# Linear attention with two gated layers: q of blocks 1 to 5 loaded in 32x32 pieces and transposed by VectorE

## The chip, the cores and the metric

The kernel runs on one core of a Trainium2 chip. The metric is the device time of one execution in microseconds. The engines are TensorE (PE, with its weight loads as PEld), VectorE (DVE), ScalarE (ACT), GpSimd (POOL) and SyncE (SP), whose queue issues all the transfers of this kernel.

## The reference

For each of 4 batches and 8 heads, k and v give a 64 x 64 matrix, q is multiplied by it, and each row is normed. The result is a matrix x of 2304 tokens x 512, which goes through a layer with a gate and then through a product of two layers:

```
kv  = einsum('bhsd,bhse->bhde', k, v)              # q, k, v: 4 x 8 x 576 x 64, float32
out = einsum('bhsd,bhde->bhse', q, kv)
out = out / sqrt(mean(out * out, -1) + 1e-6) * g_norm
x   = out.transpose(0, 2, 1, 3).reshape(2304, 512)
h   = x @ w_in;  x1 = (h * sigmoid(h)) @ w_out      # 512 -> 2048 -> 512
y   = ((x1 @ w_a) * (x1 @ w_b)) @ w_out2            # 512 -> 1536 -> 512
```

The weights come as float64 and are decoded on the chip.

## The kernel before, in words

The tokens are cut into 6 blocks of 384 (three chunks of 128). The matrix products are done at full float32 precision by splitting each operand into a high and a low part and adding three products.

A weight tile of w_in or w_out (names wi0 to wi15 and wo0 to wo15) is loaded raw (load_w, L265), scaled by ScalarE (dec_scale, L279), shifted and joined by VectorE (dec_shift L285, dec_low L291, dec_sign L298), and split into the high part (ScalarE, L307) and the low part (GpSimd or VectorE, L313).

For each block and each of 4 pairs of heads, q has to lie with the head's dimension along the partitions, since TensorE contracts over partitions. load_q (L123) loads a chunk of 128 tokens with all 8 heads, one token to a partition, in runs of 64 floats. stage_a1 (L173) has TensorE transpose the three chunks of a pair into PSUM (qtp), and stage_a2 (L180) has ScalarE copy them to SBUF (qT). stage_b (L189) multiplies qT by kvc, the matrices of k and v (ao); then come the norm (L201 to L218) and a second transpose, x, which is split into xh and xl (L224 to L240). Block 0 loads its q in another way (load_q_first, L134).

A step of the main loop (step1, L399) is one hidden tile of one block: 12 matmuls for h (hp, L328), the gate (ScalarE's sigmoid L388, VectorE's product L393), the split of the gate into gh and gl (L338, L343), and the 12 matmuls of the step before into x1 (x1p, L354). Work of the next block, the decoding of weights and the loads hang on steps (the table `side`, filled by `at`, L738); a step's extra work follows its x1 on each engine. VISITS (L42) says which hidden tiles of which block follow each other, and base[i] is the first step of visit i. q of block 2 is transposed in steps 19, 21, 23 and 25, q of blocks 3, 4 and 5 in the steps base[5], base[6] and base[7] plus 1, 4, 7 and 10.

The opening is written out by hand. LOADS (L23) is the order of the first loads in SP's queue: `q3 q4 q5` are the chunks of block 1, `k11` is k and v of batch 1 and pair 1, `t1` their last 64 tokens, `wi1` a raw weight tile. ORDER (L27) is the order of the items on all the engines: `A:1:2` is stage_a1 of block 1 and pair 2, `a:1:2` its stage_a2, `c`, `s`, `j`, `k`, `p`, `P` are the steps of a weight's decoding, `K` and `O` make kvc, `H` is a part of h, `G`, `g`, `S`, `t` gate and split, `X` is x1. Each engine works its instructions off in this order, and an instruction that waits holds up all that stand behind it on its engine.

Buffers: `page` is a pool of 37 tiles of 4 KB per partition, `small` one of 6 tiles of 2 KB.

Of the kernel before, what the change touches and what calls it, by code (L numbers as in the profile page):

```python
# [8 lines left out]
F32 = mybir.dt.float32  # L9
# [6 lines left out]
P = 128  # L16
CH = 3
TB = CH * P
# [2 lines left out]


LOADS = """  # L23
k02 Q t0 k00 k01 g k03 wi1 wi0 q3 q4 wo0 q5 wo1 k11 k10 t1 wi2 wo2 wo3 wi3 k13 k12"""


ORDER = """  # L27
W:11 Q:1 Q:0 Q:2 W:1 A:0:2 K:0:2 A:0:1 A:0:3 K:0:0 a:0:2 O:0:2:0 O:0:2:1 A:0:0 B:0:2 O:0:0:0 a:0:3 O:0:0:1 a:0:0
K:0:1 B:0:0 a:0:1 n:0:2 r:0:2 K:0:3 n:0:0 O:0:1:0 c:wi1 O:0:1:1 O:0:3:1 w:0:2 r:0:0 m:0:2 s:wi1 B:0:1 O:0:3:0 w:0:0
n:0:1 B:0:3 n:0:3 r:0:1 m:0:0 w:0:1 r:0:3 w:0:3 W:7 j:wi1 d:0:2 m:0:1 k:wi1 c:wi0 d:0:0 W:4 x:0:2 s:wi0 d:0:1 p:wi1  # L30
m:0:3 x:0:1 P:wi1 d:0:3 x:0:0 x:0:3 j:wi0 k:wi0 p:wi0 c:wo0 H:1:0:4 l:0:0 P:wi0 H:1:4:8 A:1:2 A:1:1 l:0:1 a:1:1
H:0:0:4 l:0:2 l:0:3 c:wo1 H:1:8:12 A:1:0 H:0:4:8 H:0:8:12 a:1:0 G:1 G:0 s:wo0 j:wo0 A:1:3 s:wo1 k:wo0 g:1 a:1:2
K:1:0 j:wo1 p:wo0 k:wo1 a:1:3 p:wo1 g:0 S:1 P:wo0 O:1:0:0 O:1:0:1 K:1:1 O:1:1:1 O:1:1:0 B:1:0 S:0 P:wo1 c:wi2 t:1
B:1:1 t:0 X:0:0 n:1:0 X:0:1 s:wi2 j:wi2 n:1:1 r:1:0 w:1:0 c:wo2 k:wi2 c:wo3 r:1:1 X:0:2 X:1:0 p:wi2 s:wo3 w:1:1
X:1:1 X:1:2 P:wi2 s:wo2 m:1:0 d:1:0 H:2:0:4 c:wi3 j:wo3 m:1:1 s:wi3 d:1:1 x:1:0 l:1:0 H:2:4:8 K:1:3 j:wi3 k:wo3
# [6 lines left out]
VISITS = [(0, 0, 4), (1, 0, 8), (0, 4, 12), (1, 8, 16), (0, 12, 16),  # L42
          (2, 0, 16), (3, 0, 16), (4, 0, 16), (5, 0, 16)]
# [16 lines left out]
def tile_linattn_moe_moe2(ctx: ExitStack, tc: tile.TileContext, q, k, v, g_norm,  # L60
                          w_in, w_out, w_a, w_b, w_out2, out):
    nc = tc.nc
    B, H, S, D = q.shape
# [22 lines left out]
    first = tc.alloc_tile_pool(name="first", bufs=1)  # L86
# [2 lines left out]
        return sb.tile(shape, dt, tag="page", bufs=NPAGE, name=name)  # L89

    def small(shape, dt, name):
        return first.tile(shape, dt, tag="small", bufs=6, name=name)

    def mid(shape, dt, name):
        return sb.tile(shape, dt, tag="mid", bufs=6, name=name)
# [10 lines left out]
    qs, qT, xn, ao, rms, xt = {}, {}, {}, {}, {}, {}  # L106
    xh, xl = {}, {}

    def load_kv(b, p):
        t = page([P, 2, 2, 4 * D], F32, f"kv_{b}_{p}")  # L110
        for i, src in enumerate((k, v)):
            nc.sync.dma_start(
                t[:, i], src[b, 2 * p:2 * p + 2, 0:4 * P, :].rearrange("h (p c) d -> p h (c d)", c=4))
        kvp[b, p] = t

    def load_kvt(b):
        t = page([P, 2, H, D], F32, f"kvt_{b}")
        nc.gpsimd.memset(t[ST:], 0.0)
        for i, src in enumerate((k, v)):
            nc.sync.dma_start(t[0:ST, i], src[b, :, 4 * P:S, :].rearrange("h p d -> p h d"))  # L120
        kvt[b] = t

    def load_q(c):  # L123

        t = (page if c < 2 * CH else small)([P, H, D], F32, f"q_{c}")
        done = 0
        while done < P:
            b, t0 = divmod(c * P + done, S)
            n = min(P - done, S - t0)
            nc.sync.dma_start(t[done:done + n], q[b, :, t0:t0 + n, :].rearrange("h p d -> p h d"))  # L130
            done += n
        qs[c] = t

    def load_q_first():  # L134

        t = six([P, H, CH, D], F32, "q_first")
        nc.sync.dma_start(t.rearrange("p h c d -> p h (c d)"),
                          q[0, :, 0:TB, :].rearrange("h (p c) d -> p h (c d)", c=CH))
        qs["first"] = t
# [31 lines left out]
    bufs = {"at": 2, "h": 2, "acc": 4}  # L171

    def stage_a1(j, p, tag="at"):  # L173

        pt = ps.tile([P, TB], F32, tag=tag, bufs=bufs[tag], name=f"qtp_{j}_{p}")
        for i in range(CH):
            nc.tensor.transpose(pt[:, i * P:(i + 1) * P], qs[j * CH + i][:, 2 * p:2 * p + 2, :], ident)  # L177
        qT[j, p] = pt

    def stage_a2(j, p):  # L180
        t = mid([P, TB], F32, f"qT_{j}_{p}")
        nc.scalar.copy(t, qT[j, p])
        qT[j, p] = t

    def stage_a(j, p):
        stage_a1(j, p)
        stage_a2(j, p)

    def stage_b(j, p, tag="at"):  # L189

# [60 lines left out]
    def load_w(key):  # L251
        kind, f = key
        fs = slice(f * P, (f + 1) * P)
        src = srcs[kind]
        wide = src.dtype != F32
        if kind in ("wi", "wa", "wb"):
            src = src[:, fs]
        else:
            src = src[fs, :]
        if wide:  # L260
            src = src.bitcast(U32)
        if kind in ("wi", "wa", "wb"):
            src = src.rearrange("(kt p) f -> p kt f", p=P)
        r = page([P] + list(src.shape[1:]), U32 if wide else F32, f"raw_{kind}{f}")
        nc.sync.dma_start(r, src)  # L265
        raws[key] = r.rearrange("p k f -> p (k f)") if kind in ("wi", "wa", "wb") else r
# [43 lines left out]
    def dec_rest(key, eng=None):  # L310
        m = mids.pop(key)
        hi, lo = W[key]
        (eng or nc.gpsimd).tensor_sub(lo, m, hi.bitcast(F32))  # L313
# [6 lines left out]
    acc, part, gg = {}, {}, {}  # L320
# [410 lines left out]
    base = []  # L731
    n = 0
# [5 lines left out]
    def at(g, fn, *args):  # L738
        side.setdefault(g, []).append(lambda: fn(*args))
# [20 lines left out]

    v4 = base[4]
    for p in range(NP):
        at(v4 - 9 + 2 * p, stage_a, 2, p)
        at(v4 - 8 + 2 * p, attend, 2, p)
        at(-(v4 - 7 + 2 * p), norm_mul, 2, p)
        at(v4 + p // 2, stage_d, 2, p)
    for vi in range(5, 8):
        j = VISITS[vi][0] + 1
        for p in range(NP):
            at(-(base[vi] + 3 + 3 * p), norm_mul, j, p)  # L770
            at(base[vi] + 1 + 3 * p, stage_a, j, p)
            at(base[vi] + 2 + 3 * p, attend, j, p)
            at(base[vi] + 4 + 3 * p, stage_d, j, p)
    for i in range(CH):
        at(v4 - 12 + i, load_q, 2 * CH + i)
        for vi in range(5, 8):
            at(base[vi] - 3 + i, load_q, (VISITS[vi][0] + 1) * CH + i)

    early = {}
# [111 lines left out]
    def load_g():  # L893
        nc.sync.dma_start(g2[0:D], g_norm.unsqueeze(1))
        nc.sync.dma_start(g2[D:P], g_norm.unsqueeze(1))

    for name in LOADS.split():
        if name == "g":
            load_g()
        elif name == "Q":  # L900
            load_q_first()
        elif name[0] == "t":
            load_kvt(int(name[1]))
        elif name[0] == "k":
            load_kv(int(name[1]), int(name[2]))
        elif name[0] == "q":
            load_q(int(name[1]))
        else:
            load_w((name[:2], int(name[2:])))

# [2 lines left out]
    def item(name):  # L913
        kind, *r = name.split(":")
        if kind in "csjkpPyL":
            key = (r[0][:2], int(r[0][2:]))
            if kind == "L":
                load_w(key)
            elif kind == "y":
                dec_rest(key, nc.vector)  # L920
            else:
                {"c": dec_scale, "s": dec_shift, "j": dec_low, "k": dec_sign, "p": dec_high,
                 "P": dec_rest}[kind](key)
            return
        r = [int(e) for e in r]
        early = r[0] == 0
        if kind == "W":
            warm(*r)
        elif kind == "Q":
            unpack_q(*r)  # L930
        elif kind == "K":
            kv_mm(*r)
        elif kind == "O":
            kv_out(*r)
        elif kind == "A":
            stage_a1(*r, "acc" if early else "at")
        elif kind == "a":
            stage_a2(*r)
        elif kind == "B":
            stage_b(*r, "acc" if early else "at")  # L940
        elif kind == "n":
            norm_square(*r)
        elif kind == "r":
            norm_mean(*r)
        elif kind == "w":
            norm_root(*r)
        elif kind == "m":
            norm_mul(*r)
        elif kind == "d":
            stage_d1(*r, "acc" if early else "at")  # L950
        elif kind == "x":
            stage_d2(*r)
        elif kind == "l":
            stage_d3(*r)
        elif kind == "H":
            f, n0, n1 = r
            if n0 == 0:
                hp[f] = ps.tile([P, TB], F32, tag="h", bufs=2, name=f"hp_0_{f}")
            h_part(hp[f], 0, "wi", f, n0, n1)
        elif kind == "G":  # L960
            gate1(0, r[0], hp[r[0]])
        elif kind == "g":
            gate2(0, r[0], hp[r[0]])
        elif kind == "S":
            gg[0, r[0]] = [split_high(hg[0, r[0]], f"0_{r[0]}")]
        elif kind == "t":
            gg[0, r[0]].append(split_low(hg.pop((0, r[0])), gg[0, r[0]][0], f"0_{r[0]}"))
        elif kind == "X":
            f, i = r
            if f == 0 and i == 0:  # L970
                acc[0] = [ps.tile([P, TB], F32, tag="acc", bufs=4, name=f"x1p_0_{c}") for c in range(KD)]
            for c in range(KD):
                x1_part(0, f, c, i)

    with tc.manual_schedule():
# [7 lines left out]
        g = base[1]  # L983
# [14 lines left out]
        for n, (d, p) in enumerate(seq):  # L998
            new = 0 < n < NPAIR
            if NPAIR + 1 <= n <= NPAIR + 4:  # L1000

                kt, h = divmod(n - NPAIR - 1, 2)
# [50 lines left out]
```

## Time and profile before

| | us |
|---|---|
| median of 3 runs | 881.38 (880.87 to 881.59) |
| span of the profiled execution, from the first to the last instruction | 879.4 |
| TensorE busy in the span | 869.5 |
| VectorE busy | 595.9 |
| ScalarE busy | 318.2 |
| GpSimd busy | 50.7 |

The profile gives the profiled execution as its span; a time that it took from outside is not told apart from the three runs. The first 45 us of the span are the opening, in which the DMA engines are busy over 90% of the time (the page's first two slices of 22 us). The main loop of the gate layer follows, then the product of the two layers.

### The profile page before, as it was taken

The numbers are of one execution on the slowest core, as the hardware profiler recorded it, in microseconds if no ns is written. First come the engines' busy times: TensorE is split into PE (matmuls) and PEld (weight loads), VectorE is DVE, ScalarE is ACT, GpSimd is POOL, SyncE is SP. The second block draws the span as 40 slices with busy tenths as digits, with TensorE's granted clock in tenths as the row PEclk, the third lists the DMA queues.
The fourth block names the chain that finished last, engine by engine and source line by source line (L and its number), as shares of the span: only waits on it lengthen the run. The fifth ranks groups of instructions, "written<-read, shape, count | busy, mean of one in ns | idle before, by whom it ended". The sixth has DMA issues, their size and how long they took to land.

```text
span 879.4 us, 13480 instructions
## 1 busy us (share of the span) xinstructions
PE 869.5 (99%) x5111; PEld 828.9 (94%) x5111; DVE 595.9 (68%) x1115; ACT 318.2 (36%) x648; POOL 50.7 (6%) x53
## 2 busy tenths in 40 slices
PE   8999999999999999999999999999999999999998
PEld 5799999999999999999999999999999999999996
DVE  4889786454677678888755677776656665535555
ACT  4766554343444445455442422221222211121110
POOL 4410002010101000100000000000000000000000
PEclk9999999999999999999999999999999999999999
DMA  9960244044463565558999967276788476765001
GB/s 296 368 246 1 73 140 112 1 134 157 139 218 139 182 201 186 195 220 292 407 367 374 360 238 263 97 271 256 249 289 287 132 274 240 286 216 193 1 0 72
DMA packets 99185, 179.67 MB, mean 204 GB/s; under 512 B 26544, under 2 KB 68016, under 8 KB 99120
## 3 DMA queue, kind: packets, MB, share of 16 engines
q1 hardware_dynamic: 99120, 178.81, 57.7%
q8 instruction: 40, 0.66, 0.3%
q14 instruction: 25, 0.20, 0.1%
HBM read 127.66 MB, written 51.12 MB: 203 GB/s over the span
## 4 chain that ended last, share of the span: by engine, by line
PE 96%; DVE 1%; DMA 1%; ACT 1%; issue 0%; POOL 0%; SPq 0%; DVEq 0%; ACTq 0%
PE hp L328 23%; PE x1p L354 22%; PE op L710 17%; PE X_a L632 4%; PE V_a L632 4%; PE Z_a L632 4%; PE X_b L632 4%; PE Z_b L632 4%; PE V_b L632 4%; PE Y_b L632 2%; PE Y_a L632 2%; PE ao L197 2%; DMA kv<-in_v_dram 1%; PE kvps L159 1%; PE qtp L177 1%; PE xtp L231 1%
## 5 line engine op out<-in xcount | busy, mean ns | idle before, releaser
L354 PE MATMUL x1p<-gh,wo 128*128 128x384 f32 x768 | 193.4, 335 | 0.0
L328 PE MATMUL hp<-xh,wi 128*128 128x384 f32 x768 | 154.7, 342 | 0.4 <-ACT xh L235 0.3
L354 PEld LDWEIGHTS x1p<-gh,wo 128*128 128x128 f32 x768 | 138.4, 188 | 0.0
L328 PEld LDWEIGHTS hp<-xh,wi 128*128 128x128 f32 x768 | 132.9, 188 | 1.6 <-ACT xh L235 1.0
L354 PE MATMUL x1p<-gl,wo 128*128 128x384 f32 x384 | 127.4, 335 | 0.0
L388 ACT ACTIVATE g<-hp 128x384 f32<-128x384 f32 x96 | 47.2, 491 | 113.7 <-PE hp L328 113.6
L393 DVE TENSOR_TENSOR g<-hp,g 128x384 f32<-128x384 f32 x96 | 53.3, 555 | 49.4 <-ACT g L388 49.0
L710 PE MATMUL op<-wp,ab 128*128 128x512 f32 x360 | 83.4, 390 | 0.0
L328 PE MATMUL hp<-xl,wi 128*128 128x384 f32 x384 | 82.4, 335 | 0.0
L710 PEld LDWEIGHTS op<-wp,ab 128*128 128x128 f32 x360 | 67.4, 188 | 13.7
L684 ACT CAST ab<-a 128x384 fp32r<-128x384 f32 x72 | 37.0, 514 | 115.1 <-DVE a L678 58.1
L343 DVE TENSOR_TENSOR gl<-g,gh 128x384 fp32r<-128x384 f32 x96 | 54.7, 570 | 31.3 <-ACT gh L338 27.4
L338 ACT CAST gh<-g 128x384 fp32r<-128x384 f32 x96 | 49.3, 514 | 67.5 <-DVE g L393 67.4
L718 DVE TENSOR_TENSOR o<-op,o 128x512 f32<-128x512 f32 x90 | 60.3, 686 | 17.6 <-PE op L710 17.5
L354 PEld LDWEIGHTS x1p<-gl,wo 128*128 128x128 f32 x384 | 71.9, 188 | 0.0
L328 PEld LDWEIGHTS hp<-xl,wi 128*128 128x128 f32 x384 | 67.9, 188 | 0.3 <-DVE xl L239 0.3
L710 PE MATMUL op<-w,ab 128*128 128x512 f32 x288 | 66.9, 390 | 0.0
L710 PEld LDWEIGHTS op<-w,ab 128*128 128x128 f32 x288 | 53.9, 188 | 10.9
L213 POOL TENSOR_TENSOR rr<-ss,nhalf 128x6 f32<-128x6 f32 x24 | 34.4, 1438 | 297.1 <-DVE ss L208 297.0
L632 PE MATMUL X_a<-xc,wp 128*128 128x384 f32 x216 | 43.8, 337 | 0.0
L632 PE MATMUL Z_a<-xc,wp 128*128 128x384 f32 x216 | 43.3, 335 | 0.0
L632 PE MATMUL V_a<-xc,wp 128*128 128x384 f32 x216 | 43.3, 335 | 0.0
(137 smaller groups left out, 1249.4 us busy)
## 6 DMA issues: line engine op xcount, KB each, us to landing
wp<-wd SPq DMA_DIRECT2D x114, 512.0 KB, 6.1
xc<-xcd SPq DMA_DIRECT2D x21, 768.0 KB, 7.4
raw_wi<-in_moe_w_in_dram SPq DMA_DIRECT2D x16, 512.0 KB, 7.6
raw_wo<-in_moe_w_out_dram SPq DMA_DIRECT2D x16, 512.0 KB, 7.3
raw_wa<-in_moe_w_a_dram SPq DMA_DIRECT2D x12, 512.0 KB, 5.9
raw_wb<-in_moe_w_b_dram SPq DMA_DIRECT2D x12, 512.0 KB, 5.9
wd<-s_wa SPq DMA_DIRECT2D x12, 512.0 KB, 3.3
wd<-s_wb SPq DMA_DIRECT2D x12, 512.0 KB, 3.3
```

The source lines that it names most:

```text
L197: nc.tensor.matmul(o[a:e, i], t[:, i * P + a:i * P + e], kvc[bb, p], start=True, stop=True)
L213: nc.gpsimd.tensor_tensor(r, rms[j, p], nhalf, op=ALU.pow)
L328: nc.tensor.matmul(o, w[wp][:, kt * P:(kt + 1) * P], x[key][:, kt, :], start=(n == 0), stop=(n == 3 * KD - 1))
L338: nc.scalar.copy(gh, src)
L343: nc.vector.tensor_sub(gl, src, gh.bitcast(F32))
L354: nc.tensor.matmul(acc[vi][c], w[wp][:, c * P:(c + 1) * P], gg[vi, s][g], start=(s == s0 and i == 0), stop=(s == s1 - 1 and i == 2))
L388: nc.scalar.activation(g, o, AF.Sigmoid)
L393: nc.vector.tensor_mul(g, o, g)
L632: nc.tensor.matmul(b[bank], w_part(p, mat, name, wq, kt), xc[d, i][:, xq, kt, :], start=(fresh and k == 0), stop=(k == 5), skip_group_chec ...
L684: nc.scalar.copy(o[:, 0], t)
L710: nc.tensor.matmul(o, ab[d, p, f, n][:, g, ts], wp[p, 7 + f][:, wq * DM:(wq + 1) * DM], start=(k == 0), stop=(k == 5))
L718: nc.vector.tensor_add(t, o, t)
```

## The change

q of blocks 1 to 5 is no longer loaded by chunks. For each pair of heads (r = 0, 1) and each half of the head's dimension, one part of a tile qb is loaded into 32 partitions: partition i of a part gets the tokens i, i + 32, i + 64, ... and of each 32 floats. VectorE's transpose turns each 32x32 block, and the result has the head's dimension along the partitions and the tokens in order along the row, as qT had it. A part is cut where the block crosses from one batch to the next, which blocks 1 and 4 do. q of block 0 stays as it was, and the function stage_a is gone.

```
 LOADS = """
-k02 Q t0 k00 k01 g k03 wi1 wi0 q3 q4 wo0 q5 wo1 k11 k10 t1 wi2 wo2 wo3 wi3 k13 k12"""
+k02 Q t0 k00 k01 g k03 wi1 wi0 b2 b1 wo0 b0 b3 wo1 k11 k10 t1 wi2 wo2 wo3 wi3 k13 k12"""
...
-m:0:3 x:0:1 P:wi1 d:0:3 x:0:0 x:0:3 j:wi0 k:wi0 p:wi0 c:wo0 H:1:0:4 l:0:0 P:wi0 H:1:4:8 A:1:2 A:1:1 l:0:1 a:1:1
+m:0:3 x:0:1 P:wi1 d:0:3 x:0:0 x:0:3 j:wi0 k:wi0 p:wi0 c:wo0 H:1:0:4 l:0:0 P:wi0 H:1:4:8 l:0:1 a:1:1
...
-        return first.tile(shape, dt, tag="small", bufs=6, name=name)
+        return first.tile(shape, dt, tag="small", bufs=3, name=name)
...
+    def load_q_blocks(j, p):
+        t = first.tile([P, TB // 32, 32], F32, tag="qb", bufs=4, name=f"qb_{j}_{p}")
+        for part in range(4):
+            r, half = divmod(part, 2)
+            done = 0
+            while done < TB:
+                b, t0 = divmod(j * TB + done, S)
+                n = min(TB - done, S - t0)
+                nc.sync.dma_start(
+                    t[part * 32:part * 32 + 32, done // 32:(done + n) // 32, :],
+                    q[b, 2 * p + r, t0:t0 + n, half * 32:half * 32 + 32].rearrange("(t i) d -> i t d", i=32))
+                done += n
+        qs["blocks", j, p] = t
+
+    def turn_q(j, p):
+        qT[j, p] = mid([P, TB], F32, f"qT_{j}_{p}")
+        nc.vector.transpose(qT[j, p], qs.pop(("blocks", j, p)).rearrange("p t d -> p (t d)"))
...
-        at(v4 - 9 + 2 * p, stage_a, 2, p)
+        at(v4 - 9 + 2 * p, turn_q, 2, p)
...
-            at(base[vi] + 1 + 3 * p, stage_a, j, p)
+            at(base[vi] + 1 + 3 * p, turn_q, j, p)
...
-    for i in range(CH):
-        at(v4 - 12 + i, load_q, 2 * CH + i)
+    for i in range(4):
+        at(v4 - 13 + i, load_q_blocks, 2, i)
         for vi in range(5, 8):
-            at(base[vi] - 3 + i, load_q, (VISITS[vi][0] + 1) * CH + i)
+            at(base[vi] - 4 + i, load_q_blocks, VISITS[vi][0] + 1, i)
...
-            stage_a2(*r)
+            stage_a2(*r) if early else turn_q(*r)
```

On SP's queue in the opening, between the raw tiles of w_in and k and v of batch 1, this stood before (the last number of a name is the tile's, and 128x8x64 means partitions, heads and floats):

```order
L265 DMA raw_wi1_121<-in_moe_w_in_dram 128x4x256
L265 DMA raw_wi0_123<-in_moe_w_in_dram 128x4x256
L130 DMA q_3_125<-in_q_dram 128x8x64
L130 DMA q_4_127<-in_q_dram 64x8x64 x2
L265 DMA raw_wo0_130<-in_moe_w_out_dram 128x1024
L130 DMA q_5_132<-in_q_dram 128x8x64
L265 DMA raw_wo1_134<-in_moe_w_out_dram 128x1024
L112 DMA kv_1_1_136<-in_k_dram 128x2x256
L112 DMA kv_1_1_136<-in_v_dram 128x2x256
```

This stands there now (32x6x32 means partitions, runs and floats; the line numbers are those of the changed kernel):

```order
L269 DMA raw_wi1_121<-in_moe_w_in_dram 128x4x256
L269 DMA raw_wi0_123<-in_moe_w_in_dram 128x4x256
L132 DMA qb_1_2_125<-in_q_dram 32x6x32 x8
L132 DMA qb_1_1_134<-in_q_dram 32x6x32 x8
L269 DMA raw_wo0_143<-in_moe_w_out_dram 128x1024
L132 DMA qb_1_0_145<-in_q_dram 32x6x32 x8
L132 DMA qb_1_3_154<-in_q_dram 32x6x32 x8
L269 DMA raw_wo1_163<-in_moe_w_out_dram 128x1024
L112 DMA kv_1_1_165<-in_k_dram 128x2x256
L112 DMA kv_1_1_165<-in_v_dram 128x2x256
```

Four transfers of q became 32, and raw_wo1 and all that follows stand behind them.

On VectorE in the opening, from block 0's xl (the low part of x) to the gate's low parts gl, this stood before:

```order
L239 SCALAR_TENSOR_TENSOR xl_0_317<-xtp_0_1_328,g2_64,xh_0_316 128x384
L239 SCALAR_TENSOR_TENSOR xl_0_317<-xtp_0_2_307,g2_64,xh_0_316 128x384
L239 SCALAR_TENSOR_TENSOR xl_0_317<-xtp_0_3_338,g2_64,xh_0_316 128x384
L285 TENSOR_SCALAR m_wo0_348<-m_wo0_348 128x512
L291 SCALAR_TENSOR_TENSOR m_wo0_348<-raw_wo0_130,m_wo0_348 128x512
L285 TENSOR_SCALAR m_wo1_379<-m_wo1_379 128x512
L298 SCALAR_TENSOR_TENSOR m_wo0_348<-raw_wo0_130,m_wo0_348 128x512
L393 TENSOR_TENSOR g_0_1_399<-hp_0_1_350,g_0_1_399 128x384
L291 SCALAR_TENSOR_TENSOR m_wo1_379<-raw_wo1_134,m_wo1_379 128x512
L298 SCALAR_TENSOR_TENSOR m_wo1_379<-raw_wo1_134,m_wo1_379 128x512
L393 TENSOR_TENSOR g_0_0_401<-hp_0_0_372,g_0_0_401 128x384
L343 TENSOR_TENSOR gl_0_1_462<-g_0_1_399,gh_0_1_434 128x384
```

This stands there now, from the shift of wo1 on:

```order
L140 STREAM_TRANSPOSE qT_1_0_414<-qb_1_0_145 128x384
L289 TENSOR_SCALAR m_wo0_377<-m_wo0_377 128x512
L295 SCALAR_TENSOR_TENSOR m_wo0_377<-raw_wo0_143,m_wo0_377 128x512
L289 TENSOR_SCALAR m_wo1_400<-m_wo1_400 128x512
L302 SCALAR_TENSOR_TENSOR m_wo0_377<-raw_wo0_143,m_wo0_377 128x512
L397 TENSOR_TENSOR g_0_1_416<-hp_0_1_379,g_0_1_416 128x384
L140 STREAM_TRANSPOSE qT_1_2_425<-qb_1_2_125 128x384
L295 SCALAR_TENSOR_TENSOR m_wo1_400<-raw_wo1_163,m_wo1_400 128x512
L302 SCALAR_TENSOR_TENSOR m_wo1_400<-raw_wo1_163,m_wo1_400 128x512
L140 STREAM_TRANSPOSE qT_1_3_442<-qb_1_3_154 128x384
L397 TENSOR_TENSOR g_0_0_418<-hp_0_0_393,g_0_0_418 128x384
L347 TENSOR_TENSOR gl_0_1_475<-g_0_1_416,gh_0_1_447 128x384
```

The four transposes stand among block 0's xl (one, not in these rows), ahead of the shift of wo0 (one) and behind the shift of wo1 (two). On TensorE and ScalarE the groups of three transposes and the copies of blocks 1 to 5 are gone and nothing else moved.

In the stage of block 4 the 32 pieces stand on SP's queue between raw_wb0, raw_wb1 and raw_wa2, raw_wa3, with four stores of decoded weights (wd) among them, where four transfers of q stood.

## Rows read from the trace of the kernel before

**Rows 1.** The page's busy times: engine, us (share of the span), instructions.

```profile
PE 869.5 (99%) x5111; PEld 828.9 (94%) x5111; DVE 595.9 (68%) x1115; ACT 318.2 (36%) x648; POOL 50.7 (6%) x53
```

**Rows 2.** The chain that ended last: share of the span by engine.

```profile
PE 96%; DVE 1%; DMA 1%; ACT 1%; issue 0%; POOL 0%; SPq 0%; DVEq 0%; ACTq 0%
```

**Rows 3.** TensorE's timeline, 107 to 118.5 us: start, us, engine, line, what.

```profile
109.24 0.50 PE L354 MATMUL x1p<-gh,wo 128*128 128x384 f32 x2
...
113.41 0.50 PE L354 MATMUL x1p<-gh,wo 128*128 128x384 f32 x2
...
115.48 0.49 PE L177 MATMUL qtp<-ident,q 128*128 128x128 f32 x3
...
117.90 0.50 PE L354 MATMUL x1p<-gh,wo 128*128 128x384 f32 x2
```

**Rows 4.** Groups by form: count | busy us, mean ns | idle before, releaser.

```profile
L208 DVE TENSOR_REDUCE ss<-sq 128x6 f32<-128x390 f32 x24 | 13.4, 557 | 16.1 <-ACT sq L203 16.1
...
L177 PE MATMUL qtp<-ident,q 128*128 128x128 f32 x72 | 11.8, 277 | 0.9 <-DVE q L147 0.8
...
L182 ACT COPY qT<-qtp 128x384 f32<-128x384 f32 x24 | 11.2, 475 | 2.6 <-PE qtp L177 2.4
```

**Rows 5.** VectorE's timeline, 237 to 242 us.

```profile
238.18 0.56 DVE L343 TENSOR_TENSOR gl<-g,gh 128x384 fp32r<-128x384 f32 x1
```

**Rows 6.** TensorE's timeline, 237 to 242 us.

```profile
240.10 0.34 PE L354 MATMUL x1p<-gl,wo 128*128 128x384 f32 x1
```

**Rows 7.** SP's queue in the opening: start of issue, us that it took, what.

```profile
9.60 4.84 SPq L130 DMA_DIRECT2D q<-in_q_dram  x3
...
15.96 1.16 SPq L265 DMA_DIRECT2D raw_wo<-in_moe_w_out_dram  x1
```

**Rows 8.** SP's queue at 92, 124 and 246 us: three forms of load.

```profile
92.36 0.37 SPq L130 DMA_DIRECT2D q<-in_q_dram  x1
...
124.06 0.62 SPq L120 DMA_DIRECT2D kvt<-in_k_dram  x1
...
246.15 1.32 SPq L130 DMA_DIRECT2D q<-in_q_dram  x2
```

**Rows 9.** DMA issues at 16.0 and 59.7 us: count, KB, us to landing.

```profile
raw_wo<-in_moe_w_out_dram SPq DMA_DIRECT2D x1, 512.0 KB, 6.6
...
raw_wo<-in_moe_w_out_dram SPq DMA_DIRECT2D x1, 512.0 KB, 3.5
```

**Rows 10.** ScalarE's timeline, 20 to 32 us: start, us, what [idle before, releaser].

```profile
23.71 0.67 ACT L279 ACTIVATE m_wo<-raw_wo 128x512 f32<-128x512 f32 x1
25.18 0.48 ACT L182 COPY qT<-qtp 128x384 f32<-128x384 f32 x1 [0.80 <-PE qtp L177]
...
26.61 0.49 ACT L388 ACTIVATE g<-hp 128x384 f32<-128x384 f32 x1 [0.56 <-PE hp L328]
```

**Rows 11.** VectorE's timeline, 20 to 32 us.

```profile
29.33 2.13 DVE L343 TENSOR_TENSOR gl<-g,gh 128x384 fp32r<-128x384 f32 x2 [0.75 <-ACT gh L338]
31.39 0.41 DVE L285 TENSOR_SCALAR m_wi<-m_wi 128x512 uint32<-128x512 uint32 x1
```

**Rows 12.** TensorE's timeline, 26 to 32.5 us.

```profile
29.66 2.29 PE L197 MATMUL ao<-kvc,qT 128*128 128x128 f32 x16 [0.44 <-ACT kvc L167]
31.70 1.11 PE L354 MATMUL x1p<-gh,wo 128*128 128x384 f32 x5
```

**Rows 13.** SP's queue, 238 to 252.8 us.

```profile
238.54 1.04 SPq L265 DMA_DIRECT2D raw_wb<-in_moe_w_b_dram  x2
...
251.01 1.65 SPq L265 DMA_DIRECT2D raw_wa<-in_moe_w_a_dram  x2
```

**Rows 14.** ScalarE's timeline, 268 to 270 us.

```profile
268.29 1.23 ACT L279 ACTIVATE m_wa<-raw_wa 128x512 f32<-128x512 f32 x2
```

**Rows 15.** The run's end by stretches: busy us by engine, PEclk the granted clock.

```profile
870.00:877.00 7.00, 5.52 (x25) 4.24 (x23) 3.46 (x5) 0.00 (x0) 0.00 (x0) 1.00 0.48 187
...
877.80:879.30 1.50, 0.00 (x0) 0.00 (x0) 0.00 (x0) 0.00 (x0) 0.00 (x0) 0.50 0.01 1
```

More of the change, by code (lines that the diff above doesn't have):

```diff
@@ L30 @@
 n:0:1 B:0:3 n:0:3 r:0:1 m:0:0 w:0:1 r:0:3 w:0:3 W:7 j:wi1 d:0:2 m:0:1 k:wi1 c:wi0 d:0:0 W:4 x:0:2 s:wi0 d:0:1 p:wi1
-m:0:3 x:0:1 P:wi1 d:0:3 x:0:0 x:0:3 j:wi0 k:wi0 p:wi0 c:wo0 H:1:0:4 l:0:0 P:wi0 H:1:4:8 A:1:2 A:1:1 l:0:1 a:1:1
-H:0:0:4 l:0:2 l:0:3 c:wo1 H:1:8:12 A:1:0 H:0:4:8 H:0:8:12 a:1:0 G:1 G:0 s:wo0 j:wo0 A:1:3 s:wo1 k:wo0 g:1 a:1:2
+m:0:3 x:0:1 P:wi1 d:0:3 x:0:0 x:0:3 j:wi0 k:wi0 p:wi0 c:wo0 H:1:0:4 l:0:0 P:wi0 H:1:4:8 l:0:1 a:1:1
+H:0:0:4 l:0:2 l:0:3 c:wo1 H:1:8:12 H:0:4:8 H:0:8:12 a:1:0 G:1 G:0 s:wo0 j:wo0 s:wo1 k:wo0 g:1 a:1:2
 K:1:0 j:wo1 p:wo0 k:wo1 a:1:3 p:wo1 g:0 S:1 P:wo0 O:1:0:0 O:1:0:1 K:1:1 O:1:1:1 O:1:1:0 B:1:0 S:0 P:wo1 c:wi2 t:1
@@ L121, in load_kvt @@
         kvt[b] = t
[L123 to L132, printed above, removed]
+    def load_q_blocks(j, p):
[14 more added lines that the diff above has]
+        nc.vector.transpose(qT[j, p], qs.pop(("blocks", j, p)).rearrange("p t d -> p (t d)"))
     def load_q_first():
@@ L183, in stage_a2 @@
         qT[j, p] = t
-    def stage_a(j, p):
-        stage_a1(j, p)
-        stage_a2(j, p)
     def stage_b(j, p, tag="at"):
@@ L905, in tile_linattn_moe_moe2 @@
             load_kv(int(name[1]), int(name[2]))
-        elif name[0] == "q":
-            load_q(int(name[1]))
+        elif name[0] == "b":
+            load_q_blocks(1, int(name[1]))
         else:
@@ L935, in item @@
         elif kind == "A":
-            stage_a1(*r, "acc" if early else "at")
+            stage_a1(*r, "acc")
         elif kind == "a":
-            stage_a2(*r)
+            stage_a2(*r) if early else turn_q(*r)
         elif kind == "B":
```

## The prediction

> **What bounds the kernel now.** I read the page first: TensorE is busy 99% of the span [rows 1], and the chain that ended last is TensorE for 96% of it [rows 2]. So time taken off TensorE comes off the end wherever nothing else is late, and time added elsewhere costs only where TensorE is made to wait. Then I read TensorE's timeline, which shows what one group of q transposes costs, then the timelines of SyncE's queue (SP), ScalarE and VectorE in the first 35 us, the one stretch where the other engines set TensorE's pace, and last the stage in which q of block 4 is loaded, because a queue that gets more transfers must be looked at wherever it gets them. The span of the profiled execution is 879.4 us and the median of the runs 881.4; I take the 2.0 us between them as unchanged, so a change of the span is added to 881.4.
>
> **What goes from TensorE.** A plain step of the gate/up loop, from one start of x1 to the next, lasts 113.41 - 109.24 = 4.17 us. The next step, which ends in the three transposes of one pair of heads, lasts 117.90 - 113.41 = 4.49 us [rows 3]. A group of three thus costs TensorE 0.32 us, not three times the 277 ns of one instruction, since neighbours overlap [rows 4]. The change removes 20 groups: 16 of blocks 2 to 5, in stages where TensorE has no other wait, and 4 of block 1 in the opening. The 16 give 16 x 0.32 = 5.1 us. The 4 would give 1.3 us, but they stand ahead of a wait that the change lengthens (below), so I count nothing for them.
>
> **What goes from ScalarE.** 20 copies of 475 ns [rows 4], all at places where TensorE does not wait for them except in the opening; nothing is counted.
>
> **What VectorE gets.** 20 transposes of 128x384. None is in this trace. The nearest rows are one-source instructions of the same width, 557 ns (the reduction, 128x390) [rows 4]; the ends I keep are 0.41 us, the shift over 512 columns [rows 11], and 1.11 us, twice the reduction. I take 0.56, or 0.47 start to start as its neighbours have it. In blocks 2 to 5 each stands in a step's tail, ahead of the next gate. The tightest place I found there is gl, which ends at 238.74 and is first read at 240.10: 1.36 us to spare [rows 5, 6]. That holds even 1.11 us, so the 16 cost nothing. If that cover were gone, each would cost TensorE what exceeds it.
>
> **What SyncE gets.** This is the term that decides. q of block 1 was 4 transfers; it is 32 now (4 pairs x 4 parts, and each part is cut in two where the batch changes at token 576), each of 32 partitions x 6 x 128 bytes, 24 KB. One queue issues them in order, between raw_wi0 and raw_wo1, and everything behind raw_wo1 (k and v of batch 1, the next weights) is pushed back with it. What does one issue cost? q in 128 partitions took 0.37 us when it was alone; kvt, in 64 partitions, 0.62; the q halves in 64 partitions 1.32 for two, 0.66 each [rows 8]. So fewer partitions are no cheaper here, they are dearer, although half the bytes move. For 32 partitions the trace has no row: below is 0.37 + 0.05 between issues = 0.42, above is one more step of 0.29 on top of 0.66, 0.95 + 0.05 = 1.0. I take 0.66 with the gap, the row of the same function with the smallest transfer.
>
> The opening with that: the issue of the pieces begins at 9.60, where the first q load was issued [rows 7]. 32 x 0.66 = 21.1 us, and raw_wo0 between them 0.5 (1.04 for two) [rows 13]: raw_wo1 is issued at 31.2 instead of 15.96 [rows 7]. It then landed 6.6 us after its issue, in a full queue; a raw_wo in an empty one took 3.5 [rows 9]. The queue now holds little but small pieces, so I take 4.0: it lands at 35.2. In the trace ScalarE's scaling of wo1 starts at 23.71, and VectorE's shift of wi2, behind both gl, at 31.39 [rows 10, 11]: 7.68 us, of which 0.80 + 0.56 (ScalarE for TensorE) and 0.75 us (VectorE for ScalarE) are waits that will be long over. Two of the four new transposes stand in that stretch on VectorE: 7.68 - 2.11 + 2 x 0.47 = 6.5 us. The shift comes at 35.2 + 6.5 = 41.7, which is 10.3 us late, and TensorE's x1, which started at 31.70 [rows 12], is late by as much: TensorE has finished hidden tiles 0 and 1 by then and stands still, with k and v of block 1 behind raw_wo1 as well. After that it is busy without a break, so nothing is made up. With the landing at its two ends (3.5 and 6.6) the delay is 9.8 to 12.9 us.
>
> Standing still has a second price. The granted clock went to half after TensorE's last matmul at the end of the run [rows 15], so a hole of ten microseconds in the opening will probably let it fall too. The matmuls that then resume on the path, ao, were 2.29 us [rows 12]; at half clock they cost up to 2.3 us more. I take 0, since VectorE and ScalarE pace the chain there, and keep 2.3 for the range.
>
> In the other blocks the queue has room. Block 4 is the worst, again 32 pieces: from 238.54 + 1.04, 16 x 0.66 = 10.6, then a store, 8 x 0.66, three stores (at about 0.5 each), 8 x 0.66 put the two raw_wa at 262.8 and 263.3 instead of from 251.01 [rows 13]; landing some 4.5 us later (3.5 for one alone [rows 9], the second behind it), at 268, they just meet ScalarE's scaling at 268.29 [rows 14]. No cost at 0.66; at 1.0 they would be issued from 273.6 and land some 10 us too late.
>
> Here the Trainium skill speaks against the change. In the page "DMA: Bandwidth & Descriptors", section Rules for kernel authors, it says that many small transfers should be made one large one, since below 64 KB one pays mostly overhead. Its section Bandwidth gives 0.68 us for 4 KB and 0.95 for 64 KB; by an estimate from these, 24 KB would be 0.8 us, 32 in a row 25 us, and the opening 4 us later than in my sum. The trace agrees in kind: half the bytes took longer to issue.
>
> **Sum:** +10.3 in the opening, - 5.1 in blocks 2 to 5, 0 elsewhere: +5.2, so 886.6 us.
>
> **Rivals.**
>
> *Only bytes count (faster).* If issues of 24 KB go out at 0.3 us or less, or the pieces slip in while the queue is full anyway (three q loads held SP for 4.84 us [rows 7]), raw_wo1 comes hardly later, and the opening pays only for VectorE: 4 x 0.47 less the 0.75 us that it waits at 29.33 [rows 11], 1.1 us. 1.1 - 5.1 = -4.0: 877.4. For it: 4.84 us of SP time are already lost to a full queue there. Against it: no q load of the trace was issued in less than 0.37, and 0.42 x 32 alone is 13.4 us; that gives raw_wo1 at 23.5, landing at 27.5, a delay of 2.6 and a net of -2.5 (878.9).
>
> *No change.* With 0.44 to 0.55 us per issue the opening loses 3.4 to 6.9 us and the 5.1 are just used up: 881.4. For it: 0.52 is what a 512 KB weight load costs in issue [rows 13], and the cost may not depend on partitions. Against it: the two forms with fewer partitions. It also comes out where issue costs nothing but the rate halves with the length of a piece, 256 to 128 bytes: the 4.84 us in which the three q loads held SP [rows 7] come a second time, -4.0 + 4.8 = +0.8, 882.2; for that the trace has no row, since none of its loads moves 128-byte pieces.
>
> A second rule of the Trainium skill belongs to this: the same page, section Specifications, has 512 bytes as the least length at line rate and says that below it the DMA reads, modifies and writes. No run here shows 128-byte pieces yet; q's 256-byte pieces were below it already.
>
> *Two places instead of one (much slower).* At 1.0 us per issue raw_wo1 is issued at 42.1, the opening loses 21 us, and block 4 another 9 (10 less what the slack of 1.36 us holds): +21 + 9 - 5 = +25, 906. It begins to decide at about 0.7, where raw_wa of block 4 lands after its scaling. For it: the step from 128 to 64 partitions. Against: 128 to 64 may be one step between two forms and not a slope.
>
> **How the numbers follow.** Forecast (0.55 to 0.8 per issue, 883 to 892) 0.50; much slower 0.14; no change 0.16; faster 0.20. A difference below 0.2% (1.8 us) can't be told from none. Faster by more 0.20, within 0.16, slower 0.64. The range leaves out a tenth on each side: below, half of the faster cases; above, most of the two-place case. 878 to 897; the forecast's own range is 883 to 892.
>
> **What would show it.** SP: 32 issues of qb between raw_wi0 and raw_wo1, near 0.6 us each, and raw_wo1 near 31. ScalarE: a wait for raw_wo before the scaling of wo1, until about 35. TensorE: a hole of some 10 us before kvps of block 1, its granted clock possibly at half behind it; x1 first at about 42; then steps that last 4.17 where they lasted 4.49, with no wait. VectorE: STREAM_TRANSPOSE near 0.5 us. The prediction is wrong if the issues take under 0.45, if x1 starts before 36, or if TensorE waits between 260 and 300 us (raw_wa) or for qT.

## The result, and the profile after

The changed kernel took 886.86 us (median of 4 runs, 884.56 to 888.37), the kernel before 881.39 in the same comparison: a ratio of 1.0059, 95% interval 1.0047 to 1.0071. It is slower by 5.5 us; 886.6 was predicted. The profiled execution took 886.85 us with a span of 885.0, 5.6 longer than before.

The page's busy times and the shares of the chain that ended last [rows 1, 2]:

```profile
PE 867.6 (98%) x5051; PEld 826.0 (93%) x5051; DVE 605.8 (68%) x1135; ACT 310.3 (35%) x628; POOL 50.6 (6%) x53
...
PE 95%; DMA 2%; SPq 2%; DVE 0%; ACT 0%; issue 0%
```

TensorE's busy time is 1.9 us less although it lost 20 groups of transposes; something made other matmuls longer. SyncE's queue (SPq) and DMA, 1% before, now hold 4% of the chain.

The gain shows in TensorE's timeline, in the step of block 2 that [rows 3] shows before:

```profile
124.60 0.51 PE L358 MATMUL x1p<-gh,wo 128*128 128x384 f32 x2
...
128.77 0.50 PE L358 MATMUL x1p<-gh,wo 128*128 128x384 f32 x2
```

4.17 us from x1 to x1 where it was 4.49, with no wait in it. The loss lies ahead of that. The queue in the opening (start of issue, us, what), which answers to [rows 7]:

```profile
9.95 9.51 SPq L132 DMA_DIRECT2D qb<-in_q_dram  x16
19.50 0.45 SPq L269 DMA_DIRECT2D raw_wo<-in_moe_w_out_dram  x1
19.99 7.70 SPq L132 DMA_DIRECT2D qb<-in_q_dram  x16
27.73 0.44 SPq L269 DMA_DIRECT2D raw_wo<-in_moe_w_out_dram  x1
28.21 0.43 SPq L112 DMA_DIRECT2D kv<-in_k_dram  x1
```

The second 16 take 7.70 us, 0.48 each from start to start. An issue by itself took 0.44 us (the median of the 32), and so it did for what stands behind them: 0.44 for raw_wo1, 512 KB in 128 partitions, and 0.43 for k, 256 KB in 128. The first 16 take 1.8 us more, because two of them waited for the two raw_wi ahead (issuer, releaser, us in total, times, longest):

```profile
SPq L132 <- DMA raw_wi<-in_moe_w_in_dram: 1.9, 2, 1.1
```

In none of the eleven traces of this case does a transfer of SyncE's queue start before the eighth transfer ahead of it has landed. Here the piece that starts at 13.75 is the eighth behind wi1, which landed at 13.73, and the next, at 15.14, the eighth behind wi0, which landed at 15.13. raw_wo1 is issued at 27.73; it was 15.96. The chain at that place (start us, us, what) goes through the next four loads, k and v of batch 1:

```profile
29.20 0.47 SPq L112
29.71 6.21 DMA kv<-in_v_dram
35.92 0.14 issue
36.06 2.59 PE kvps L167 x40
38.65 3.86 PE ao L201 x16
42.51 5.24 PE x1p L358 x24
```

ScalarE and VectorE (against [rows 10, 11]) wait for wo1 first, but are done with it in time:

```profile
31.56 0.66 ACT L283 ACTIVATE m_wo<-raw_wo 128x512 f32<-128x512 f32 x1 [7.58 <-DMA raw_wo<-in_moe_w_out_dram]
```

```profile
32.25 0.43 DVE L289 TENSOR_SCALAR m_wo<-m_wo 128x512 uint32<-128x512 uint32 x1 [4.76 <-ACT m_wo L283]
...
40.18 0.43 DVE L289 TENSOR_SCALAR m_wi<-m_wi 128x512 uint32<-128x512 uint32 x1
```

And TensorE, against [rows 12], with its clock by stretches (the number after the five engines is the granted clock, as in [rows 15]):

```profile
36.06 1.13 PE L167 MATMUL kvps<-kv 128*64 128x64 f32 x16 [9.33 <-DMA kv<-in_v_dram]
...
38.58 3.93 PE L201 MATMUL ao<-kvc,qT 128*128 128x128 f32 x16
42.16 2.79 PE L358 MATMUL x1p<-gh,wo 128*128 128x384 f32 x8
```

```profile
7.20:31.00 23.80, 16.86 (x160) 12.98 (x160) 13.35 (x26) 9.22 (x21) 8.27 (x6) 1.00 0.70 193
31.00:44.70 13.70, 8.64 (x64) 7.38 (x65) 10.34 (x17) 7.46 (x18) 5.04 (x4) 0.50 1.07 353
44.70:60.00 15.30, 15.17 (x124) 13.28 (x122) 11.91 (x21) 8.15 (x19) 8.52 (x7) 1.00 1.06 400
```

TensorE stood still for 9.33 us; at 31.0 us, within this hole, the clock fell to the lower of its two levels (1.2 GHz), and ao took 3.93 us where it had taken 2.29. The next row of x1 is late by 42.16 - 31.70 = 10.5 us, and from step 5 of the main loop on every step starts 11.2 later than before; the 16 steps of blocks 2 to 5 then give back 5.5.

The transposes, by form (count | busy us, mean ns | idle before), are what was assumed, 0.57 us:

```profile
L140 DVE STREAM_TRANSPOSE qT<-qb 128x384 f32<-128x384 f32 x20 | 11.4, 571 | 1.1 <-DMA qb<-in_q_dram 1.0
```

### The profile page after: what moved, and what is told of

The parts are those of the page before. It is cut to its first block, busy times and chain, and to the rows that moved or that the text cites. A ratio compares the mean times of both kernels' runs of the same rounds, so it can differ in the third digit from the quotient of the medians.

```text
span 885.0 us, 13486 instructions
## 1 busy us (share of the span) xinstructions
PE 867.6 (98%) x5051; PEld 826.0 (93%) x5051; DVE 605.8 (68%) x1135; ACT 310.3 (35%) x628; POOL 50.6 (6%) x53
## 4 chain that ended last, share of the span: by engine, by line
PE 95%; DMA 2%; SPq 2%; DVE 0%; ACT 0%; issue 0%
PE x1p L358 23%; PE hp L332 22%; PE op L714 17%; PE X_a L636 4%; PE Z_a L636 4%; PE V_a L636 4%; PE Z_b L636 4%; PE V_b L636 4%; PE X_b L636 4%; PE Y_a L636 2%; PE Y_b L636 2%; PE ao L201 2%; SPq L132 1%; PE kvps L167 1%; PE xtp L235 1%; DMA kv<-in_v_dram 1%
```

## The experiments

Nine kernels were run. Step 5 of the main loop is the first one behind the disturbed opening; its start (52.98 us in the kernel before) tells the opening's loss apart from the gain later.

**Block 1 as before, blocks 2 to 5 new.**

```
-... wi1 wi0 b2 b1 wo0 b0 b3 wo1 k11 ...
+... wi1 wi0 q3 q4 wo0 q5 wo1 k11 ...
+            stage_a1(*r, "acc" if early else "at")    # block 1: TensorE
+            stage_a2(*r)                              # and ScalarE again
```

> Block 1's q is loaded and turned as in the kernel before (three loads in the opening, TensorE's transposes, ScalarE's copies); blocks 2 to 5 keep the 32x32 pieces and VectorE's transposes. Theory (the loss is SyncE's 32 issues ahead of wo1 and of batch 1's k and v): the opening ends as before, step 5 starts at about 53.0 us and not 64.2, and the gain of blocks 2 to 5 stands alone: 881.4 - 5.5 = 875.9 us (875 to 877). Rival (the loss in the opening has another cause, such as the smaller pool of work tiles or another set order, and block 1's q only falls into the same stretch): step 5 starts late by several us, 879 or more.

Measured: 875.32 us (875.22 to 875.39), ratio 0.9935 (0.9922 to 0.9947). Step 5 starts at 52.88, the clock stays at 1.0. The whole loss sits in block 1's q; the rest of the change is worth 5.8 us and costs nothing. This is the best version.

**Twice the issues, same bytes.**

```
-                n = min(TB - done, S - t0)
+                n = min(TB - done, S - t0, 96 if j == 1 else TB)
```

> The changed kernel with each of block 1's 32 loads cut in two or more (at most 96 tokens in one where there were up to 192): about 64 issues for the same 786 KB in the same 128-byte pieces. Theory (a price per issue, 0.485 us from start to start in the changed kernel): 32 x 0.485 = 15.5 us more in SyncE's queue, and about 902 us. Rival 1 (a price per piece or per byte): the queue takes as long as before, 886.9 us, within 2. Rival 2 (part per issue, part per piece): between, and the start-to-start time of one issue falls from 0.485 us by as much.

**Half the issues, same bytes.**

```
-                b, t0 = divmod(j * TB + done, S)
+                b, t0 = divmod((0 if j == 1 else j) * TB + done, S)
```

> The changed kernel, but block 1 reads the q of block 0's 384 tokens, which lie in one batch: so 16 loads of 48 KB in place of 32 of 24 KB, with the same bytes and the same 128-byte pieces. Block 1's output is that of other tokens; the work is the same. Theory (a price per issue): 16 x 0.485 = 7.8 us less in SyncE's queue ahead of wo1, k and v; step 5 starts about 8 us earlier than in the changed kernel (64.2), and the time is 878 to 879 us. Rival (a price per piece or per byte): the queue is as long, 886.9 us, within 2.

Measured: 900.73 us (899.45 to 903.29) with 64 issues, ratio 1.0219 (1.0203 to 1.0234); 880.77 (879.18 to 881.40) with 16, ratio 0.9996 (0.9987 to 1.0005). The second row of pieces in each queue, 64 issues first, and then the first row of the one with 16:

```profile
28.00 15.37 SPq L132 DMA_DIRECT2D qb<-in_q_dram  x32
```

```profile
17.84 4.18 SPq L132 DMA_DIRECT2D qb<-in_q_dram  x8
```

```profile
9.94 7.35 SPq L132 DMA_DIRECT2D qb<-in_q_dram  x8
```

15.37 us for 32 of 12 KB and 4.18 for 8 of 48 KB: 0.48 and 0.52 us each, over a fourfold range of sizes. So the price is one per issue where nothing else holds the queue. With 64 issues the theory came out (about 902 us). With 16 it did not, 880.77 and not 878 to 879: the first eight, behind the two raw_wi, took 7.35 us, 0.92 each, so raw_wo1 was issued 5.7 us earlier (22.07) and not 7.8, and step 5 started at 58.38, 5.8 earlier than in the changed kernel. The end moved by 13.9 us for 32 more and by 6.1 for 16 fewer, 0.43 and 0.38 each: most of an issue's price reaches the end. A price per piece or byte, which would have left both at 886.9, is out.

**Block 1's loads behind the urgent ones.**

```
-... wi0 b2 b1 wo0 b0 b3 wo1 k11 k10 t1 wi2 wo2 wo3 wi3 k13 k12
+... wi0 wo0 wo1 k11 k10 t1 wi2 b0 b1 wo2 wo3 wi3 k13 k12 b3 b2
-... l:0:1 a:1:1 ...          (and a:1:0, a:1:2, a:1:3 in the two lines below)
+... a:1:0 a:1:1 B:1:0 ...  a:1:3 B:1:3 ...  a:1:2 B:1:2
```

> The changed kernel with block 1's 32 loads moved behind wo0, wo1, batch 1's first k and v and wi2 (16 of them before wo2, 16 at the end of the opening's list), and each of VectorE's four transposes moved to just before the product that reads it. Theory (the issues cost only what stands behind them in SyncE's queue): VectorE and PE find wo1, k, v and wi2 where the kernel before had them, the first x1 product starts at 32 to 33 us, and the time is 875 to 877 us. Rival (the pieces of 32x32 cost in the opening wherever they stand, since wo2, wo3, wi3 and the later k and v are as urgent): the wait moves to one of these, 880 to 887 us.

Measured: 882.31 us (881.50 to 884.22), ratio 1.0018 (1.0009 to 1.0027). The theory's 875 to 877 was wrong. k and v came in time (kvps at 26.55), and TensorE waited for something else. TensorE, VectorE and ScalarE at that place:

```profile
30.99 3.93 PE L201 MATMUL ao<-kvc,qT 128*128 128x128 f32 x16 [3.05 <-ACT kvc L175]
```

```profile
29.47 0.55 DVE L397 TENSOR_TENSOR g<-hp,g 128x384 f32<-128x384 f32 x1
29.93 1.11 DVE L140 STREAM_TRANSPOSE qT<-qb 128x384 f32<-128x384 f32 x2
30.97 1.45 DVE L347 TENSOR_TENSOR gl<-g,gh 128x384 fp32r<-128x384 f32 x2
```

```profile
29.58 0.62 ACT L311 CAST wo<-m_wo 128x512 fp32r<-128x512 f32 x1 [1.92 <-DVE m_wo L302]
...
30.73 0.32 ACT L175 COPY kvc<-kvps 64x64 f32<-64x64 f32 x2
```

Two things end together at 31.0: the transposes on VectorE, and ScalarE's copies of kvc, which stand behind a cast of wo1 that waited for VectorE too. VectorE was busy for 9.9 of the 10 us from 20 to 30. A hole of 3.05 us opens on TensorE, which has no transposes of its own left to do in that time, and ao is at half clock again. A second wait, for a transpose, follows, with a mean granted clock of 0.71 from 45 to 50 us:

```profile
47.37 2.12 PE L201 MATMUL ao<-kvc,qT 128*128 128x128 f32 x8 [1.50 <-DVE qT L140]
```

Two suspects were new: VectorE, whose time I had costed at nothing in blocks 2 to 5 but which is full here, and the clock. They were taken apart.

**VectorE's transposes alone, without any loads.** The best version, with idle transposes.

```
+            nc.vector.transpose(mid([P, TB], F32, f"z_{r[1]}"), zs)    # item z
-... l:0:1 a:1:1 ...   H:0:8:12 a:1:0 ...   g:1 a:1:2 ...   k:wo1 a:1:3
+... l:0:1 z:1:1 a:1:1 ...   H:0:8:12 z:1:0 a:1:0 ...   g:1 z:1:2 a:1:2 ...   k:wo1 z:1:3 a:1:3
```

> The best so far (block 1's q by TensorE and ScalarE, blocks 2 to 5 new; 875.3 us) with four idle 128x384 transposes added on VectorE at the four places where the changed kernel has block 1's; nothing reads them. It prices VectorE's part of the opening alone, without loads. Theory: VectorE is the full engine there (12.7 us busy in 12.6 of the stretch ahead of step 2), so 4 x 0.47 to 0.57 us come through in part: 0.5 to 2.2 us, 875.8 to 877.5 us. Rival 1 (VectorE has room; only the loads cost): 875.3, within 0.4. Rival 2 (VectorE's part is most of the 11 us): 880 or more.

Measured: 880.02 us (878.85 to 880.77), +4.7 over the version without them, above the theory's range. VectorE's gl and TensorE's ao and x1, without the idle transposes:

```profile
29.24 2.13 DVE L358 TENSOR_TENSOR gl<-g,gh 128x384 fp32r<-128x384 f32 x2 [0.76 <-ACT gh L353]
```

```profile
29.58 2.29 PE L212 MATMUL ao<-kvc,qT 128*128 128x128 f32 x16 [0.22 <-ACT kvc L186]
31.62 1.67 PE L369 MATMUL x1p<-gh,wo 128*128 128x384 f32 x8
```

and with them:

```profile
32.50 1.78 DVE L358 TENSOR_TENSOR gl<-g,gh 128x384 fp32r<-128x384 f32 x2 [0.17 <-ACT gh L353]
```

```profile
32.85 3.13 PE L212 MATMUL ao<-kvc,qT 128*128 128x128 f32 x16 [2.23 <-ACT kvc L186]
35.63 2.43 PE L369 MATMUL x1p<-gh,wo 128*128 128x384 f32 x8
```

gl is 3.26 us later. In this profile 1.07 of that was there already at step 1, ahead of the first idle transpose (wi1 landed at 15.30 and not at 14.08); the other 2.2 come with the 4 transposes, 0.55 for each, about as long as one takes. Then ao lost 0.84 and x1 0.76 to the clock.

**The clock, held in three versions** by idle 128x512 matmuls in TensorE's hole: in the changed kernel (40 ahead of kvps), in the one just shown (9 ahead of ao), and in one whose 32 loads are spread (12 ahead of ao). In the changed kernel:

```
-K:1:0 j:wo1 p:wo0 ...
+W:40 K:1:0 j:wo1 p:wo0 ...
```

> The changed kernel with 40 idle 128x512 matmuls on TensorE placed in the hole ahead of batch 1's k and v (26.7 to 36.1 us), so that the engine is not idle there. Theory (the half clock from 31.0 to 44.7 us follows from the hole and costs about 3 us: kvps 0.4, ao 1.5, x1 1.1): the clock stays at 1.0 to step 2, the time is 884 us, and the runs spread by less than the 3.8 us of the changed kernel. Rival (such matmuls do not hold the clock, or it costs nothing since VectorE sets the end of that stretch): 886.9 us, within 1.

Measured: 884.89 us (883.97 to 887.13), ratio 1.0043 (1.0029 to 1.0056), clock 1.0 from 27 to 46 us:

```profile
37.68 0.69 PE L167 MATMUL kvps<-kv 128*64 128x64 f32 x16 [1.27 <-DMA kv<-in_v_dram]
...
39.93 2.29 PE L201 MATMUL ao<-kvc,qT 128*128 128x128 f32 x16 [0.19 <-ACT kvc L175]
```

From kvps to step 2 it takes 46.55 - 37.68 = 8.9 us; the changed kernel took 47.84 - 36.06 = 11.8. So half clock had cost 2.9 us. In this profile 1.6 of that was lost again, since the first 16 pieces were held longer (11.35 us and not 9.51; wi1 landed at 15.44) and raw_wo1 was issued at 29.29. The smaller spread of the runs that I expected did not come (3.2 us against 3.8).

In the version with the idle transposes:

```
-... O:1:1:0 B:1:0 S:0 ...
+... O:1:1:0 W:9 B:1:0 S:0 ...
```

> The kernel with four idle VectorE transposes beside block 1's q on TensorE (880.0 us, +4.7 over the one without them), with 9 idle 128x512 matmuls on TensorE in the 2.2 us in which it waits ahead of ao. Theory (of the 4.7 about 2 are the transposes on a full VectorE, 1.6 the half clock behind the wait, 1.1 a later landing of the first wi): 877.5 to 878.5 us at a clock of 1.0. Rival (all of it is VectorE's time): 880, within 0.5.

Measured: 877.56 us (877.02 to 878.04), ratio 0.9961 (0.9948 to 0.9973). 2.5 us come back with the clock at 1.0. What stays over 875.32 is 2.2: VectorE's four transposes, and a part that the later landing of the first wi has in it (0.8 us in this profile, by the start of step 1).

**Block 1's loads spread two by two between the large ones,** without and then with the idle matmuls.

```
-... wi1 wi0 wo0 wo1 k11 k10 t1 wi2 b0 b1 wo2 ...
+... wi1 b00 wi0 b01 wo0 b02 wo1 b03 k11 b10 k10 b11 t1 b12 wi2 b13 wo2 b30 ...   (b01: pair 0, part 1)
```

> As the kernel with block 1's loads moved back (882.3 us), but its 32 loads stand two by two between the large loads of the opening and not in two rows of 16. Theory (a small load costs 0.485 us of SyncE's queue while it moves only 0.2 us of the transfer engines' work, so what is lost is the time in which 16 small ones in a row leave the engines idle; between large loads, where SyncE waits for landings anyway, they cost only the 0.2 us): wo2, wo3, k and v come 3 to 5 us earlier than in the two rows, step 5 starts at 55 to 58 us in place of 61.0, and the time is 877 to 879 us. Rival (32 issues cost their 0.485 us each wherever they stand in the opening): 882 us, within 1.

Measured: 881.77 us (877.64 to 883.08), ratio 1.0000 (0.9988 to 1.0012): by the median the rival. But the runs differ by their mean granted clock: 877.64 us at 1.000, 879.22 at 0.998, 880.38 at 0.998, 880.7 and 881.1 at 0.996, and 881.8 to 883.1 at 0.991 to 0.994. So the clock was held here too, and the fourth transpose was moved up, ahead of the product of pair 3:

```
-... a:1:0 a:1:1 B:1:0 ...   K:1:2 a:1:3 B:1:3 ...   G:2 a:1:2 B:1:2
+... a:1:0 a:1:1 W:12 B:1:0 ...   K:1:2 a:1:3 a:1:2 B:1:3 ...   G:2 B:1:2
```

> The kernel with block 1's loads spread two by two (881.8 us median, runs from 877.6 at a mean granted clock of 1.0 to 883.1 at 0.991), with 12 idle 128x512 matmuls on TensorE in the 3.05 us in which it waits for block 1's two transposes, and the fourth transpose moved from behind wo2's decoding on VectorE to right behind the third. Theory (the spread loads cost little, and what is left is the half clock that follows TensorE's wait, 1.6 us in ao, 1.2 in x1 and some more after the second wait of 1.5): clock 1.0, runs close together, 876.5 to 878 us. Rival (the half clock goes along with the loss but is not its cause): 881 to 882 us, with the same spread.

Measured: 877.89 us (877.13 to 879.17), ratio 0.9965 (0.9951 to 0.9978). Two things were changed at once, but the version without them had one run at a clock of 1.000, and that run took 877.64, which speaks for the clock as what came back.

```profile
28.32 2.54 PE L890 MATMUL warm<-wz 128*128 128x512 bf16 x11 [0.16 <-issue]
31.21 2.29 PE L202 MATMUL ao<-kvc,qT 128*128 128x128 f32 x16 [0.36 <-DVE qT L141]
33.25 1.66 PE L359 MATMUL x1p<-gh,wo 128*128 128x384 f32 x8
```

With the clock held, 32 spread loads and VectorE's transposes (877.89) cost 0.3 us more than the idle transposes without loads (877.56). The comparison has one more difference, TensorE's transposes of block 1, which only the latter has; at the 0.32 us of a group they are worth up to 1.3 us, so the 32 spread loads cost between 0.3 and 1.6 us. In two rows ahead of what is urgent they made most of the 11.5 us (half clock included) between the changed kernel and the best version.

Whether two rows of 16 behind the urgent loads cost more than the spread is not shown, since no run has them with the clock held. Without that, the medians are 882.31 and 881.77, and the stretch from step 1 to step 5 took 36.88 us at a mean granted clock of 0.81 in the one profile and 35.62 at 0.86 in the other: 29.9 and 30.6 us in terms of the full clock, by estimate, so the clock can be all of the difference. What a row of small pieces does to the transfers shows in the stretch from 24.8 to 30.4 us of the version with the loads moved back (the last three columns are the clock, the transfer engines' busy share and GB/s):

```profile
24.80:30.40 5.60, 3.14 (x50) 2.75 (x49) 5.53 (x9) 2.32 (x5) 1.39 (x2) 0.97 0.29 46
```

While SyncE issues only small pieces, the transfer engines are busy 29% of the time and move 46 GB/s; with large loads in the queue it is 400 (the changed kernel from 44.7 us on).

## Why the prediction was right

The mechanism was right: the issues of block 1's pieces in SyncE's queue hold up what stands behind them, as the runs with 16 and 64 issues show. That the time was right within 0.3 us is luck. The price of an issue was too high, which is worth 5.6 us, and the terms that were left out or too small are worth 5.9, net of a gain that was larger by 0.4.

- **Gain in blocks 2 to 5:** 5.1 predicted, 5.5 by the starts of steps in the profile, 5.8 by the version with block 1 as before.
- **VectorE's transposes:** 0.56 us predicted, 0.57 measured; free in blocks 2 to 5, as predicted. In the opening, where VectorE is full, they cost about 0.5 us each once the loads are out of the way. In the changed kernel that does not show: VectorE waits there for wo1, and its second gl is done at 40.17, 2 us before x1 starts.
- **Price of an issue:** mis-sized, 0.66 predicted and 0.485 measured. I had read "fewer partitions, dearer" from kvt and the q halves in 64 partitions; in 32 partitions an issue took 0.44 us, as in 128 (raw_wo1). Why the loads in 64 take longer (kvt 0.63 in the changed kernel too) stays open. The lower bound, 0.42, was nearer. raw_wo1 was issued at 27.73 and not 31.2. By 0.485 alone it would have been 25.6; the rest is a queue that starts 0.35 later and is held by the landings of wi1 and wi0 during the first 16 pieces (9.51 us and not 7.8), which I had not counted. By the Trainium skill's page "DMA: Bandwidth & Descriptors", section Bandwidth, I had estimated 0.8 us; its figures are for loads in 128 partitions that GpSimd issued, in time of the transfer engines, so they price something other than an issue from SyncE, and here the measurement decides. The rule that I took from the Trainium skill (same page, section Rules for kernel authors: make many small transfers one large one) agrees with the runs: half the issues gave 6.1 us.
- **What ends last:** the prediction followed raw_wo1 through ScalarE and VectorE, and named k and v behind it only in passing. By that chain VectorE's shift of wi2 would have come 6.5 us after wo1's landing; it came 40.18 - 31.54 = 8.6 after. TensorE's wait ended with v of pair 0, issued four loads later and landing at 35.92, 4.4 us after wo1: in a queue that filled again it took 6.2 us.
- **Half clock:** taken as 0, with 2.3 as its bound. It cost 2.9 us: ao 1.6, less than the 2.3 that I had as its most, and x1 and kvps the rest, which I had not counted.
- **Signs of being wrong:** "under 0.45 us" was at its edge, 0.44 for an issue by itself and 0.485 from start to start. x1 did not start before 36. Block 4 cost nothing, as predicted: its two raw_wa were issued 21.6 us after raw_wb (24.3 predicted), at 0.52 to 0.60 us for a piece, and landed by 273.8, ahead of their scaling at 276.3; the profile shows no wait of TensorE from 245 to 310 us.

```profile
268.54 0.94 SPq L269 DMA_DIRECT2D raw_wa<-in_moe_w_a_dram  x2
```

With 0.485 us per issue and nothing else changed the sum would have been 881.0 (landing 29.6, shift of wi2 at 36.1, + 4.7 - 5.1). What brought the time back to 886.9 are the terms that I had left out: the late and held queue (2.1), the half clock (2.9) and what is left, 1.3 with the gain at 5.5, for the later landing of v. x1's start at 42.16 (42.0 predicted) hides that. The rival "no change" had its condition met (0.44 to 0.55 us per issue) and was still wrong, because its sum lacked the same terms.

What stays open: why wi0 and wi1 land up to 1.7 us later in some traces than in others (wi1 at 13.73 in the changed kernel and at 15.44 in the same kernel with idle matmuls, both with the same loads), which moves the whole opening. Each version's trace is one execution.

## What to carry to other kernels

A queue that issues in order charged here per transfer, not per byte: count the issues ahead of whatever is urgent, don't put a row of small loads there, and try them one or two at a time between the large ones, where 32 of them cost 0.3 to 1.6 us. A move from one engine to another is free only in the stretches in which the new engine has room, so price the stretches apart and keep the change where it pays (here blocks 2 to 5 alone: 0.9935, interval 0.9922 to 0.9947, against 1.0059 for all). And a hole of a few microseconds on TensorE is paid twice, once as the wait and once as the slower matmuls behind it; where it can't be closed, idle matmuls in it gave 2.0 and 2.5 us back, and 3.9 together with one transpose moved.

## What the runs showed of the hardware

- An issue from SyncE took 0.43, 0.44 and 0.47 us for 12, 24 and 48 KB in 32 partitions (the second rows of the runs with 64, 32 and 16 issues), and 0.44 for 512 KB in 128 partitions right behind them; alone in the queue, 256 KB in 128 partitions took 0.37 [rows 8].
- No transfer of SyncE's queue started before the eighth ahead of it had landed, in any of the eleven traces (435 to 562 transfers each); in each, 16 to 35 started within 0.05 us of that landing. So a late large load holds up small ones behind it: 9.51 us for the first 16 pieces, 7.70 for the second.
- Small loads of 12, 24 and 48 KB that stood in a full queue landed as close as 0.16 to 0.2 us to each other, with 128-byte pieces: the transfer engines were not what limited them in the opening (0.48 us from issue to issue). A piece of 128 bytes kept a transfer engine for 13 ns, one of 256 for 18, one of 1024 for 46 and one of 4096 for 159 (medians, changed kernel): the same bytes cost 1.4 times as much in pieces of 128 as of 256, and there is no jump in these.
- The clock was at half not only behind TensorE's hole of 9.33 us but also behind waits of 2.23 and 3.05 us; in the version with the loads spread, with its wait of 3.05, it was so in some executions and not in others, and the runs of one kernel went from 877.6 us at a mean clock of 1.000 to 883.1 at 0.994.
